# Moving the pooling additions of the values from VectorE to GpSimd in an attention and feed-forward kernel

## The chip, the cores and the metric

The kernel runs on one core of one Trainium2 chip. The metric is device time in microseconds, from the start of the program to its end. The kernel before takes 893.63 us, the median of three runs between 892.76 and 893.68 us. Engines are named as the profile names them: PE (TensorE), DVE (VectorE), ACT (ScalarE), POOL (GpSimd) and SP (SyncE, which only issues DMAs here).

## The reference

Inputs are q, k and v of shape 8 x 8 x 576 x 64 (batches, heads, positions, width of a head), and two weight matrices of 512 x 2048 and 2048 x 512.

```
k_p = k.reshape(B, H, Sp, 8, D).mean(axis=3)        # 72 pooled keys per head
v_p = v.reshape(B, H, Sp, 8, D).mean(axis=3)        # 72 pooled values per head
scores = scale * matmul(q, k_p^T); attn = softmax(scores)
x = matmul(attn, v_p)                               # laid out as 4608 tokens x 512
h = x @ w_in;  g = h * clip(h + 3, 0, 6) / 6;  out = g @ w_out
```

The step that the change is about is the mean over 8 neighbouring positions of the values: 72 pooled positions, each the sum of 8 rows of 64 numbers. (A factor of 1/8 is put in later.)

## The kernel before, in words

The 4608 tokens are cut into twelve blocks. The feed-forward part of a block fills PE almost without a pause: first the products with w_in (lines L841 and L1134), then the gate on ACT and DVE (L849 to L861, L1090 to L1098), then the products with w_out (L872, L1188, L1261), whose inputs are split in a high and a low part (L1113 on ACT, L1115 on DVE). Blocks 0 to 3 run one by one; from block 4 on, two blocks at a time form a super block, which streams its weights from DRAM (`chunk`, L980 to L994, seven buffers, five chunks ahead). Attention for a later block is done in small steps in between (`Paced`, L893 to L916): the next block's x has to be there when its turn comes.

Attention of a tile of 128 tokens and four heads takes this chain: the scores (PE, L463), their maximum (DVE, L467), four exponentials with sums (ACT, L472), the inverse of the sums (DVE, L489 and L490), the division (POOL, `divide`, L501 and L507), the transposition of the result (PE, L572 and L574), copies out of PSUM (ACT L583, L596, DVE L585, L598), and at last the product with the pooled values (PE, `av`, L646).

A batch's values are prepared by `side_steps(b)`: six loads (`load_v`), two for each of three pieces, and three calls of `prep_v(b, p)` with p = 0, 2 and 4. The pieces with p = 0 and 2 hold the first 64 pooled positions of two pairs of heads (128 partitions); the piece with p = 4 holds the remaining 8 positions of all heads (96 partitions, three small loads from `vr_l` for each half). The two halves x and y of a piece are 512 numbers per partition each. `prep_v` makes three additions, each of which reads what the one before it wrote: x += y (512 numbers), then the left half of x gets the right half added (256), then once more (128). After that ACT writes the high part of the pooled values (L395 for p = 0 and 2, L409 for p = 4) and DVE the low part (L396, L410). The loads go into a ring of four buffers, shared with the keys (`ring`, L163); a load waits until the operations that read the buffer before are done.

Two things set the order of the work. The text `ORDER` fixes each engine's order for the part of the program up to the start of block 1, in which no value of batch 2 or later is pooled. Behind it a scheduler places each instruction in its engine's queue; `mark` and `after_mark` keep side work on an engine behind the main chain's last marked instruction there. `mark` is called behind instructions of DVE, ACT and SP, and behind none of POOL. Each engine works through its queue in order, so an instruction that waits holds up all behind it.

Of the kernel before, what the change touches and what calls it, by code (L numbers as in the profile page):

```python
# [13 lines left out]
ALU = mybir.AluOpType  # L14
# [84 lines left out]
def attention_moe_kernel(  # L99
# [19 lines left out]
    nc = tc.nc  # L119
# [63 lines left out]
    def after_mark():  # L183

        if len(window) == 2 and traced[-1].engine in marks:
            behind(traced[-1], marks[traced[-1].engine])
# [141 lines left out]
    class FirstValues:  # L328
# [19 lines left out]
        def place_heads(self):  # L348
            for h in range(2):
                rows = slice(h * D, (h + 1) * D)  # L350
                nc.scalar.mul(self.v32[rows, :, h * D : (h + 1) * D], self.ps[rows], 1.0 / POOL)
# [14 lines left out]
    def place_v(b):  # L366

        W[b] = (
            pool.tile([P, NPAIR, 2 * D], F32R, name="vhi", bufs=2),
            pool.tile([P, NPAIR, 2 * D], F32R, name="vlo", bufs=2),  # L370
            pool.tile([3 * REM, NG, 4 * D], F32R, name="vrem", bufs=2),
        )
        for w in W[b][:2]:
            nc.gpsimd.memset(w.bitcast(F32), 0.0)

    def prep_v(b, p):

        if p == 0 and b not in W:
            place_v(b)
        n = P if p < NPAIR else 3 * REM  # L380
        x, y = (vraw.pop((b, p + i))[:n, : POOL * D].rearrange("p (c n) -> p c n", c=2) for i in range(2))
        for w, a, c in ((4 * D, x, y), (2 * D, x, x[:, :, 2 * D :]), (D, x, x[:, :, D:])):
            nc.vector.tensor_tensor(out=x[:, :, :w], in0=a[:, :, :w], in1=c[:, :, :w], op=ALU.add)  # L383
            after_mark()
        if p < NPAIR:
            place_heads(b, x[:, :, :D], slice(p, p + 2))
        else:
            place_rest(b, x[:, :, :D])
# [16 lines left out]
    def place_rest(b, vs):  # L405
        lo = slice(REM, 2 * REM)
        for h in range(4):
            to, own = W[b][2][:, :, h * D : (h + 1) * D], mask[:NR, 2 + h : 3 + h]
            nc.scalar.mul(to, vs[:NR], own)  # L409
            nc.vector.scalar_tensor_tensor(  # L410
                out=to[lo],
                in0=vs[lo],
                scalar=own[lo],
                in1=to[lo].bitcast(F32),
                op0=ALU.mult,
                op1=ALU.subtract,
            )
# [238 lines left out]
    def side_steps(b):  # L656

        ks = [lambda p=p: load_k(b, p) for p in range(NPAIR)]
        ks += [lambda p=p: prep_k(b, p) for p in range(NPAIR)]
        vs = []  # L660
        n = NPAIR + NG
        for p in range(n):
            vs.append(lambda p=p: load_v(b, p))
            if p > 2 and p % 2:
                vs.append(lambda p=p: prep_v(b, p - 3))
        vs.append(lambda: prep_v(b, n - 2))
        return ks, vs
# [635 lines left out]
    a = [Step(first, f, 0, 2) for f in range(SPLIT)]  # L1303
# [33 lines left out]
    b = [Scores(t, g) for g in range(NG) for t in B]  # L1337
# [229 lines left out]
```

## Time and profile before

| | before |
|---|---|
| median of the runs | 893.63 us (892.76 to 893.68) |
| the profiled execution | 893.88 us |
| its span, first to last instruction | 892.1 us |
| TensorE clock granted | 1.00 |

The profiled execution is 0.25 us over the median, and 1.8 us of it lie outside the span. The rows of the trace that the prediction uses are shown there. A row of a group gives its number of instructions, their busy time in us and the mean of one in ns; behind the second bar stands how long the engine sat idle just before them, and what ended that. A row of a line gives minimum, median and maximum in ns. A row of the timeline gives start and length in us from the span's start, and in square brackets the idle time before. A row of waits gives the sum in us, how often, and the longest.

### The profile page before, as it was taken

How to read it: one execution, taken by the hardware profiler on the slowest of the kernel's cores; microseconds unless marked ns; L12 is line 12 of the kernel's file. 1: busy time of each engine (PE TensorE's matmuls, PEld its weight loads, DVE VectorE, ACT ScalarE, POOL GpSimd, SP SyncE). 2: the span in 40 equal slices, each digit the busy share in tenths (PEclk: the TensorE clock that was granted, in tenths of full speed). 3: DMA queues.
4: the chain of work that ended last, by engine and by line, in shares of the span. 5: the costliest groups of instructions: out<-in, count | busy, mean ns of one | idle time of the engine just before them, and what ended most of it. 6: DMA issues, size and time to landing. Idle time of an engine off the chain costs nothing.

```text
span 892.1 us, 15646 instructions
## 1 busy us (share of the span) xinstructions
PE 869.2 (97%) x5360; PEld 812.3 (91%) x5360; DVE 665.9 (75%) x1340; ACT 553.6 (62%) x1515; POOL 83.6 (9%) x168
## 2 busy tenths in 40 slices
PE   7899999999999999999999999999999999999998
PEld 6788888988989998998888999999999999999998
DVE  6999864567877785869788688897597877466664
ACT  5998766655656655778344688665577746355442
POOL 4100002110211100102000101100100200000000
PEclk9999999999999999999999999999999999999999
DMA  9970205995425234996587968877976777877873
GB/s 294 392 293 1 72 24 192 360 327 167 130 67 160 71 129 135 368 315 225 180 271 239 383 218 295 265 239 236 331 250 213 226 233 240 275 253 238 266 264 132
DMA packets 124654, 200.00 MB, mean 224 GB/s; under 512 B 13216, under 2 KB 81056, under 8 KB 124576
## 3 DMA queue, kind: packets, MB, share of 16 engines
q1 hardware_dynamic: 124432, 199.00, 67.8%
q8 instruction: 43, 0.70, 0.3%
q14 instruction: 35, 0.29, 0.1%
q10 hardware_dynamic: 144, 0.00, 0.0%
HBM read 158.08 MB, written 40.89 MB: 223 GB/s over the span
## 4 chain that ended last, share of the span: by engine, by line
PE 80%; DVE 8%; DMA 5%; ACT 4%; issue 2%; SPq 1%; POOL 0%; DVEq 0%; ACTq 0%; POOLq 0%
PE psx L1134 22%; PE psx L1261 19%; PE pso L872 12%; PE psh L841 12%; PE psx L1188 7%; PE psa L646 3%; PE psa L463 3%; ACT e L472 2%; PE psa L572 1%; DMA raw<-w_in_l 1%; DMA raw<-w_out_l 1%; DMA wd<-wq 1%; DVE vst L383 1%; DMA wsFalse<-wd 1%; DVE wq L939 1%
## 5 line engine op out<-in xcount | busy, mean ns | idle before, releaser
L1134 PE MATMUL psx<-x,wsFalse 128*128 128x384 f32 x768 | 151.8, 341 | 1.7 <-DVE g L1098 0.8
L841 PE MATMUL psh<-xhi,w 128*128 128x384 f32 (+2 forms) x520 | 145.9, 340 | 0.5 <-DVE g L853 0.4
L1134 PEld LDWEIGHTS psx<-x,wsFalse 128*128 128x128 f32 x768 | 133.6, 188 | 3.2 <-ACT c L1107 1.3
L1113 ACT CAST part<-g 128x768 fp32r<-128x768 f32 x100 | 83.3, 836 | 85.0 <-PE psx L1261 65.8
L1115 DVE TENSOR_TENSOR part<-g,part 128x768 fp32r<-128x768 f32 x100 | 95.2, 955 | 46.5 <-ACT part L1113 46.1
L872 PE MATMUL pso<-w,ghi 128*128 128x512 f32 x384 | 120.7, 398 | 0.4 <-ACT o L877 0.4
L1134 PE MATMUL psx<-x,wsTrue 128*128 128x384 f32 x576 | 115.8, 342 | 2.4 <-DMA wsTrue<-wd 2.3
L1261 PE MATMUL psx<-wsFalse,part 128*128 128x256 f32 x864 | 108.3, 282 | 1.5 <-DVE part L1115 1.1
L1261 PEld LDWEIGHTS psx<-wsFalse,part 128*128 128x128 f32 x864 | 105.2, 189 | 2.3 <-DVE part L1115 1.3
L1134 PEld LDWEIGHTS psx<-x,wsTrue 128*128 128x128 f32 x576 | 99.6, 188 | 3.1 <-DVE g L1092 3.1
L841 PEld LDWEIGHTS psh<-xhi,w 128*128 128x128 f32 x520 | 93.2, 188 | 8.2 <-DVE g L853 1.1
L472 ACT ACTIVATE e<-psa,mx 128x72 f32<-128x72 f32 x256 | 78.6, 324 | 23.7 <-DVE mx L467 22.4
L841 PE MATMUL psh<-xlo,w 128*128 128x384 f32 (+2 forms) x260 | 87.1, 336 | 0.0
L501 POOL TENSOR_TENSOR a<-e,sm 128x256 f32<-128x256 f32 x60 | 41.0, 683 | 478.3 <-DVE sm L490 377.9
L1261 PE MATMUL psx<-wsTrue,part 128*128 128x256 f32 x648 | 81.3, 283 | 0.0
L1261 PEld LDWEIGHTS psx<-wsTrue,part 128*128 128x128 f32 x648 | 79.3, 191 | 0.2 <-DVE part L1115 0.2
L872 PEld LDWEIGHTS pso<-w,ghi 128*128 128x128 f32 x384 | 69.1, 188 | 11.2 <-ACT o L877 0.7
L1090 ACT ACTIVATE r<-g,small 128x384 f32<-128x384 f32 x96 | 58.8, 621 | 28.4 <-DVE g L1098 28.0
L872 PE MATMUL pso<-w,glo 128*128 128x512 f32 x192 | 74.4, 399 | 0.0
L1098 DVE TENSOR_TENSOR g<-psx,c 128x384 f32<-128x384 f32 x96 | 52.3, 553 | 28.7 <-PE psx L1134 20.6
L1107 ACT COPY c<-psx 128x384 f32<-128x384 f32 x96 | 45.0, 485 | 28.5 <-PE psx L1134 28.1
L1092 DVE SCALAR_TENSOR_TENSOR g<-r,g 128x384 f32<-128x384 f32 x96 | 54.5, 576 | 9.7 <-ACT r L1090 9.2
(139 smaller groups left out, 1473.2 us busy)
## 6 DMA issues: line engine op xcount, KB each, us to landing
wsFalse<-wd SPq DMA_DIRECT2D x64, 512.0 KB, 4.6
wsTrue<-wd SPq DMA_DIRECT2D x48, 512.0 KB, 4.9
wsFalse<-w2d SPq DMA_DIRECT2D x31, 512.0 KB, 5.0
wsFalse<-w2t SPq DMA_DIRECT2D x27, 512.0 KB, 5.0
wsTrue<-w2d SPq DMA_DIRECT2D x21, 512.0 KB, 5.0
wsTrue<-w2t SPq DMA_DIRECT2D x21, 512.0 KB, 4.9
raw<-w_in_l SPq DMA_DIRECT2D x16, 512.0 KB, 8.6
raw<-w_out_l SPq DMA_DIRECT2D x16, 512.0 KB, 9.2
```

The lines of the kernel that those rows point to most:

```text
L472: nc.scalar.activation(self.e[:, h], self.ps[:, h], AF.Exp, bias=self.mx[:, h : h + 1], accum_out=self.sm[:, h : h + 1])
L841: nc.tensor.matmul(self.ps, l[f][:, c, :], r[:, c, :], start=c == 0 and i == 0, stop=c == NCC - 1 and i == 2)
L872: nc.tensor.matmul(pos, l, r, start=f == 0 and i == 0, stop=f == NF - 1 and i == 2)
L1090: nc.scalar.activation(r, src, AF.Relu, bias=half_low, scale=GSCALE / (6.0 * WSCALE))
L1092: nc.vector.scalar_tensor_tensor(out=g_of[i][:, k], in0=r, scalar=GSCALE, in1=src, op0=ALU.min, op1=ALU.mult)
L1098: nc.vector.tensor_tensor(out=g_of[i][:, k], in0=ps, in1=kept, op=ALU.add)
L1107: nc.scalar.copy(c, ps)
L1113: nc.scalar.copy(t[:, 0], src)
L1115: nc.vector.tensor_tensor(out=t[:, 1], in0=src, in1=t[:, 0].bitcast(F32), op=ALU.subtract)
L1134: nc.tensor.matmul(ps, w[:, l, c * P : (c + 1) * P], t[:, r, c], start=o in (1, 2, 5) and c == 0 and k == 0, stop=c == 1 and k == 2, skip_ ...
L1188: nc.tensor.matmul(to, l, w[:, qs, r], start=f == 0 and k == 0, stop=end and k == 2)
L1261: nc.tensor.matmul(to, t[:, l, k, i * P : (i + 1) * P], w[:, k, r], start=begin and k == 0 and y == 0 and i % 2 == 0, stop=m == NM - 1 and ...
```

## The change: which engine makes the additions

For batches 3 to 7 (b > 2) the three additions of `prep_v` are given to POOL, and not to DVE. Batch 0 has its own code, batch 1 is pooled by `pool_second`, and batch 2 goes on as before. These are 5 batches with 3 pieces of 3 additions, 45 instructions. Nothing else in the text changes. Lines behind L383 have a number greater by one in the changed kernel (the addition is L384, the division L502, a product with the pooled values L647).

```
         for w, a, c in ((4 * D, x, y), (2 * D, x, x[:, :, 2 * D :]), (D, x, x[:, :, D:])):
-            nc.vector.tensor_tensor(out=x[:, :, :w], in0=a[:, :, :w], in1=c[:, :, :w], op=ALU.add)
+            engine = nc.gpsimd if b > 2 else nc.vector
+            engine.tensor_tensor(out=x[:, :, :w], in0=a[:, :, :w], in1=c[:, :, :w], op=ALU.add)
             after_mark()
```

Since POOL has no mark, `after_mark` ties these additions to nothing. The scheduler moves other instructions too, on all engines, from the place on where batch 3 is pooled.

The first place is POOL's queue where the values of batch 6 (the seventh) are pooled, around the place where the super block of blocks 6 and 7 goes over from its products with w_in to those with w_out. `vst` is a buffer of values, `a` and `ar` are what a division writes, `qt` a buffer of queries that is cleared. Before:

```order
L240 MEMSET qt 128x4x64
L501 TENSOR_TENSOR a<-e,sm 128x256
L507 TENSOR_TENSOR ar<-e,sm 128x64
L501 TENSOR_TENSOR a<-e,sm 128x256
L507 TENSOR_TENSOR ar<-e,sm 128x64
L501 TENSOR_TENSOR a<-e,sm 128x256
L507 TENSOR_TENSOR ar<-e,sm 128x64
L240 MEMSET qt 128x4x64
```

And after the change:

```order
L384 TENSOR_TENSOR vst<-vst 128x512
L384 TENSOR_TENSOR vst<-vst 128x2x128
L384 TENSOR_TENSOR vst<-vst 128x2x64
L240 MEMSET qt 128x4x64
L502 TENSOR_TENSOR a<-e,sm 128x256
L508 TENSOR_TENSOR ar<-e,sm 128x64
L502 TENSOR_TENSOR a<-e,sm 128x256
L508 TENSOR_TENSOR ar<-e,sm 128x64
L384 TENSOR_TENSOR vst<-vst 96x512
L384 TENSOR_TENSOR vst<-vst 96x2x128
L384 TENSOR_TENSOR vst<-vst 96x2x64
L502 TENSOR_TENSOR a<-e,sm 128x256
```

The additions of the piece p = 2 stand ahead of the clearing and two divisions, those of the remainder (96 partitions) ahead of the third division.

The second place is PE's queue a little later, where the first product with batch 6's values is made (`psx` is a sum of the feed-forward part, `psa` one of attention, `vrem` holds the remainder's pooled values). Before:

```order
L646 MATMUL psa<-ahi,vhi 128x384
L646 MATMUL psa<-alo,vhi 128x384
L646 MATMUL psa<-ahi,vlo 128x384
L1261 MATMUL psx<-wsTrue,part 128x256 x36
L1261 MATMUL psx<-wsFalse,part 128x256 x22
L646 MATMUL psa<-arem,vrem 128x384
L1261 MATMUL psx<-wsFalse,part 128x256 x15
```

And after the change:

```order
L647 MATMUL psa<-ahi,vhi 128x384
L647 MATMUL psa<-alo,vhi 128x384
L647 MATMUL psa<-ahi,vlo 128x384
L1262 MATMUL psx<-wsTrue,part 128x256 x19
L647 MATMUL psa<-arem,vrem 128x384
L1262 MATMUL psx<-wsTrue,part 128x256 x17
L1262 MATMUL psx<-wsFalse,part 128x256 x24
```

The product with the remainder stands 19 matmuls of the feed-forward part behind the first three, and not 58. On DVE the four low parts of the remainder (L410, now L411) stand ahead of the last three gates of the super block, and before they stood behind these and three splits. On SP the remainder's second half is loaded five loads of weights earlier in the queue.

The third place is PE's queue in block 3, where a tile's scores (L463, now L464) and the transposition of the same tile (L572, now L573) stand. Before, 24 matmuls of L841, 11 of L872 and 4 of other tiles' scores stand between the two; the last twelve rows of it are

```order
L872 MATMUL pso<-w_431,glo 128x512
L841 MATMUL psh<-xhi,w_614 128x384
L841 MATMUL psh<-xlo,w_614 128x384
L841 MATMUL psh<-xhi,w_614 128x384 x2
L841 MATMUL psh<-xlo,w_614 128x384
L841 MATMUL psh<-xhi,w_614 128x384 x2
L841 MATMUL psh<-xlo,w_614 128x384
L841 MATMUL psh<-xhi,w_614 128x384 x2
L841 MATMUL psh<-xlo,w_614 128x384
L841 MATMUL psh<-xhi,w_614 128x384
L872 MATMUL pso<-w_486,ghi 128x512 x2
L572 MATMUL psa<-ident,a 128x128 x2
```

After the change these rows are all that stands between the tile's scores and its transposition, with the transposition as the last:

```order
L842 MATMUL psh<-xlo,w_344 128x384
L842 MATMUL psh<-xhi,w_344 128x384 x2
L842 MATMUL psh<-xlo,w_344 128x384
L842 MATMUL psh<-xhi,w_344 128x384
L842 MATMUL psh<-xlo,w_486 128x384
L842 MATMUL psh<-xhi,w_486 128x384 x2
L842 MATMUL psh<-xlo,w_486 128x384
L842 MATMUL psh<-xhi,w_486 128x384 x2
L842 MATMUL psh<-xlo,w_486 128x384
L842 MATMUL psh<-xhi,w_486 128x384
L464 MATMUL psa<-kbd_84,qt 128x144 x4
L573 MATMUL psa<-ident,a 128x128 x2
```

These are 13 matmuls of the feed-forward part and 4 of scores.

## Prediction

> **What bounds the kernel now.** I read the page first.
>
> ```profile
> span 892.1 us, 15646 instructions
> PE 869.2 (97%) x5360; PEld 812.3 (91%) x5360; DVE 665.9 (75%) x1340; ACT 553.6 (62%) x1515; POOL 83.6 (9%) x168
> PE 80%; DVE 8%; DMA 5%; ACT 4%; issue 2%; SPq 1%; POOL 0%; DVEq 0%; ACTq 0%; POOLq 0%
> ```
>
> PE bounds it: it is busy in 869.2 of 892.1 us, and the change takes no matmul away. All that it can win is idle time of PE, 22.9 us, and of that only what comes of DVE and lies where the values of batch 3 and later are pooled. So the second view is the waits of PE. I leave out those of the first 45 us, which the change doesn't reach.
>
> ```profile
> PE psx L1134 <- DMA wsTrue<-wd: 2.3, 1, 2.3
> PE psa L463 <- DVE arem L598: 1.3, 3, 0.9
> PE psx L1261 <- DVE part L1115: 1.1, 1, 1.1
> PE psx L1134 <- DVE g L1098: 0.8, 1, 0.8
> PE psa L646 <- DVE alo L585: 0.7, 3, 0.3
> PE psa L572 <- POOL a L501: 0.7, 1, 0.7
> PE psh L841 <- DVE g L853: 0.4, 1, 0.4
> ```
>
> The longest, 2.3 us, is a load of weights, which the change doesn't touch. The five rows with DVE hold 4.3 us: this is the whole prize. The third view, the timeline at these waits, tells whether the additions on DVE cause them. Here is DVE at the first one,
>
> ```profile
> 414.99 0.68 DVE L383 TENSOR_TENSOR vst<-vst 128x512 f32<-128x512 f32 x1
> 416.48 0.69 DVE L383 TENSOR_TENSOR vst<-vst 96x512 f32<-96x512 f32 x1 [0.81 <-DMA vst<-vr_l]
> 417.40 0.29 DVE L598 TENSOR_TENSOR arem<-psa,arem 32x128 fp32r<-32x128 f32 x1
> ```
>
> and PE there and at two others:
>
> ```profile
> 417.74 0.76 PE L463 MATMUL psa<-kbd,qt 128*128 128x144 f32 x4 [0.90 <-DVE arem L598]
> 564.43 0.96 PE L1134 MATMUL psx<-x,wsFalse 128*128 128x384 f32 x4 [0.84 <-DVE g L1098]
> 581.63 2.04 PE L1261 MATMUL psx<-wsFalse,part 128*128 128x256 f32 x15 [1.07 <-DVE part L1115]
> ```
>
> At 417.74 PE waits 0.90 us for a low part that DVE could not make, since an addition ahead of it stood 0.81 us for its load and then took 0.69 us. The other two lie beside the additions of batch 6:
>
> ```profile
> 561.08 1.10 DVE L383 TENSOR_TENSOR vst<-vst 128x512 f32<-128x512 f32 x1
> 563.04 0.41 DVE L383 TENSOR_TENSOR vst<-vst 128x256 f32<-128x256 f32 x1
> 572.31 0.69 DVE L383 TENSOR_TENSOR vst<-vst 96x512 f32<-96x512 f32 x1 [3.57 <-DMA vst<-vr_l]
> 579.46 1.13 DVE L410 SCALAR_TENSOR_TENSOR vrem<-vst,small,vrem 32x128 fp32r<-32x128 f32 x4
> ```
>
> The wait of 0.84 us follows two additions of 1.51 us together in DVE's queue. The one of 1.07 us comes 9 us after DVE stood still for 3.57 us with a load, with the splits that PE needs queued behind.
>
> **The change, part by part.** *What DVE loses.* The additions by shape:
>
> ```profile
> L383 DVE TENSOR_TENSOR vst<-vst 128x512 f32<-128x512 f32 x12 | 9.1, 762 | 0.1
> L383 DVE TENSOR_TENSOR vst<-vst 128x256 f32<-128x256 f32 x12 | 5.0, 418 | 0.1
> L383 DVE TENSOR_TENSOR vst<-vst 128x128 f32<-128x128 f32 x12 | 3.4, 284 | 0.0
> L383 DVE TENSOR_TENSOR vst<-vst 96x512 f32<-96x512 f32 x6 | 4.1, 684 | 4.4 <-DMA vst<-vr_l 4.4
> ```
>
> Three additions of 128 partitions are 0.76 + 0.42 + 0.28 = 1.46 us; 10 such pieces and 5 of 96 partitions (about as long) make some 15 x 1.46 = 21.9 us off DVE's 666. The waits for loads, 4.4 us in two places, both of batches 5 and 6, go from DVE to POOL as well. Since PE is the bound, the 21.9 us count only through the waits above.
>
> *What POOL gains.* The nearest additions of POOL are those of batch 0, on 32 partitions, and the divisions:
>
> ```profile
> L357 POOL TENSOR_TENSOR stage<-stage x3: 447/715/1252, 11.9 to 14.8; 32x512 f32<-32x512 f32 x1, 32x256 f32<-32x256 f32 x1, 32x128 f32<-32x128 f32 x1
> L501 POOL TENSOR_TENSOR a<-e,sm x60: 612/614/1313, 130.2 to 704.1; 128x256 f32<-128x256 f32 x60
> ```
>
> Upper end: 1.25 + 0.72 + 0.45 = 2.41 us a piece. Lower end: the division's 614 ns for 256 numbers, taken as 0.6 for 256, 1.2 for 512 and 0.3 for 128, gives 2.15. I take 2.41, from the same operation: 15 x 2.41 = 36 us, on an engine that is busy for 84 of 892. A piece's chain grows by 2.41 - 1.46 = 0.95 us.
>
> *Who waits for the longer chain.* For batches 3, 4, 5 and 7 nobody, I think: a batch's values are used some microseconds after they are there. Batch 6 is the close one; it is a rival below. Behind the additions in POOL's queue stand the divisions, which lead to a transposition on PE; an addition that waits for its load would hold them up. For batch 6 POOL has room:
>
> ```profile
> 545.59 0.39 SPq L284 DMA_DIRECT2D vst<-v_l  x1
> DMA to landing us min/median/max: 1.8/4.5/8.6
> 558.30 0.31 POOL L240 MEMSET qt<- 128x256 f32 x1 [11.28 <-PE psa L463]
> ```
>
> The last load of the piece p = 2 is issued at 545.59 and lands about 550.1 (median 4.5 us). DVE begins to add at 561.08, because of its queue; POOL is idle for 11.28 us before 558.30 and can add at once. The ring's buffer comes free sooner, so the load of the remainder, which waits for it, is issued sooner too, as SP's new order has it. On SP the weights of five loads stand behind that one; they are asked for five chunks ahead (18 matmuls each, at 2.04 / 15 = 0.136 us about 2.4 us, so 12 us), which hides a wait of a few.
>
> *The shared lock.* Does POOL slow DVE down? The trace shows that it does, with operations that read two inputs from SBUF:
>
> ```profile
> 635.50 0.61 POOL L501 TENSOR_TENSOR a<-e,sm 128x256 f32<-128x256 f32 x1 [3.93 <-ACT r L1090]
> 635.52 1.01 DVE L1092 SCALAR_TENSOR_TENSOR g<-r,g 128x384 f32<-128x384 f32 x1 [0.18 <-ACT r L1090]
> L1092 DVE SCALAR_TENSOR_TENSOR g<-r,g x96: 522/556/1012, 354.9 to 828.6; 128x384 f32<-128x384 f32 x96
> L1092 DVE SCALAR_TENSOR_TENSOR g<-r,g 128x384 f32<-128x384 f32 x96 | 54.5, 576 | 9.7 <-ACT r L1090 9.2
> L1098 DVE TENSOR_TENSOR g<-psx,c x96: 527/557/560, 352.3 to 827.3; 128x384 f32<-128x384 f32 x96
> ```
>
> A gate that starts 0.02 us after a division lasts 1.01 us where the median is 0.556; L1098, which has one of its inputs in PSUM, never exceeds 0.560. All 96 gates lose 96 x (0.576 - 0.556) = 1.9 us. With 36 us more of POOL they and the splits lose a few more, far less than the 21.9 us that DVE is freed of. For PE's share I bound it by 0 and by one long addition in full, 1.25 us, at a place where PE waits for DVE, and take 0.5.
>
> [...]
>
> *The scheduler's new order.* At the third place of the change's rows, a tile's transposition moves close to its scores. In the trace that tile's chain runs so:
>
> ```profile
> 276.55 0.68 PE L463 MATMUL psa<-kbd,qt 128*128 128x144 f32 x4
> 280.43 0.61 POOL L501 TENSOR_TENSOR a<-e,sm 128x256 f32<-128x256 f32 x1 [17.50 <-DVE sm L490]
> ```
>
> What PE has between the two is in the new order 13 matmuls of L841, which the chain of waits shows with their time,
>
> ```profile
> 339.52 2.10 PE psh L841 x12
> ```
>
> and 0.65 us of other scores: 13 x 2.10 / 12 + 0.65 = 2.9 us. The scores end at 277.23, the division at 281.04: 3.8 us. It waits 0.9 us if the chain is as slow as this, nothing if it is 2.9 us; I take 0.7, since only queueing on DVE can be saved.
>
> **The sum**, from the profiled execution's 893.88 us: the wait of 0.90 goes (-0.90), that of 0.84 goes (-0.84), that of 1.07 half, as DVE now has the remainder's low parts (L410) ahead of the gates and still waits for the load (-0.54), the gate's 0.4 half (-0.20); the transposition +0.7, the lock +0.5. Together -1.3: 892.6. The profiled execution is 0.25 us over the median of 893.63, so the runs' median becomes 892.4. About 0.2%, 1.8 us, is what a measurement can tell from no change; the forecast lies within it.
>
> **The rivals.** *All DVE waits go.* DVE is freed of 21.9 us and of 4.4 us of waiting at loads, and new waits don't come: -0.90 - 0.84 - 1.07 - 0.4 = -3.2 us, 890.4; with L585's 0.7 889.7. For it: in each of the places additions stand ahead. Against: the scheduler used the room to move attention forward.
>
> *The remainder of batch 6 comes too late* (slower). The matmuls ahead of PE's product with it, and the low part (ACT's share of it) that the product reads:
>
> ```profile
> 572.85 4.68 PE L1261 MATMUL psx<-wsTrue,part 128*128 128x256 f32 x36
> 576.62 1.28 ACT L409 ACTIVATE vrem<-vst,small 96x128 fp32r<-96x128 f32 x4 [0.80 <-DVE vst L383]
> ```
>
> The product now stands 19 matmuls of 4.68 / 36 = 0.13 us behind 572.85, at about 575.3. In the trace DVE's first low part is there at 579.46 + 1.13 / 4 = 579.7. If the load comes no sooner and the chain takes 0.95 us longer, PE waits 5.4 us, 4.3 more than the 1.07 that it replaces: 898.0 by the median; half of it gives 895.8. It decides when the load lands: the additions take 2.41 us, ACT's round and DVE's first low part 1.28 + 0.28 = 1.6, so it must land before 571.3, 1.0 us sooner than DVE's wait ended (572.31). Against it: POOL can add p = 2 ten microseconds sooner.
>
> *The lock* (slower). If every long addition holds a gate or split for all its time, DVE loses 36 us for 21.9 saved. Where it is nearly full, that shows:
>
> ```profile
> 240.00:260.00 20.00, 19.30 (x105) 17.19 (x104) 17.85 (x54) 12.78 (x52) 3.71 (x6) 1.00 0.29 74
> ```
>
> The pairs are busy time and instructions of PE, PEld, DVE, ACT and POOL: DVE has 2.15 us of slack there; two pieces add 1.9 us net and eat it. I price it at 1 us in this stretch and in the next like it (360 to 380 us): +2.2 with what the gates lose elsewhere, 895.8. The point is 2 us more DVE time in such a stretch.
>
> **How the numbers follow.** Forecast 0.42 (892.4, own range 891.9 to 894.5); all waits go 0.38; the remainder 0.12; the lock 0.08. So faster 0.38, same 0.42, slower 0.20. The range reaches from 889.7 of the second case to 896.0, past both slower cases at their halves.
>
> **What would show it.** Right: POOL near 120 us, DVE near 645 to 650, no DVE wait for `vr_l`, PE's waits at 417, 564 and 581 gone or smaller, the transposition near 280 waiting for POOL by under 1 us, L1092 with more long ones. Wrong: PE waiting over 2 us at the remainder's product near 575; additions of 512 numbers far from 1.25 us; DVE's sum not falling; or another wait for weights.

## The result, and the profile after

The changed kernel is slower: 898.13 us in the median of 7 runs (896.36 to 900.50), against 893.63 us in 7 runs of before (891.55 to 895.72). The ratio is 1.0059, with a 95% interval of 1.0044 to 1.0074, so 3.9 to 6.6 us lost. The forecast was 892.4 us, in a range of 889.7 to 896.0. Its profiled execution took 896.36 us, the fastest of the seven.

The first lines of the page after:

```profile
span 894.6 us, 15588 instructions
PE 871.3 (97%) x5360; PEld 813.5 (91%) x5360; DVE 663.3 (74%) x1295; ACT 553.1 (62%) x1515; POOL 125.1 (14%) x213
```

POOL has 41.5 us more, but DVE is only 2.6 us below the 665.9 of before, though 45 additions have left it. And PE, which has the same matmuls, is busy for 2.1 us longer. The two have different causes. DVE's first: these are the groups by shape (count, then busy time and mean in ns).

```profile
L384 POOL TENSOR_TENSOR vst<-vst 128x512 f32<-128x512 f32 x10 | 13.6, 1363 | 36.6 <-DMA vst<-v_l 17.6 <-DVE g L1093 8.6 <-DVE wq L945 8.1
L384 POOL TENSOR_TENSOR vst<-vst 128x256 f32<-128x256 f32 x10 | 9.6, 961 | 0.6
L384 POOL TENSOR_TENSOR vst<-vst 128x128 f32<-128x128 f32 x10 | 5.4, 537 | 0.7
L1093 DVE SCALAR_TENSOR_TENSOR g<-r,g 128x384 f32<-128x384 f32 x96 | 62.2, 657 | 11.6 <-ACT r L1091 11.2
```

The 96 gates with two inputs in SBUF take 657 ns on average, 576 before: 7.8 us more on DVE. Other operations of DVE have grown too; summed one by one, all that stayed on it takes 13.2 us more than before. POOL's additions are longer too, 2.86 us for three and not 2.41. So the two engines hold each other up far more than forecast: 14 of the 96 gates took over 0.75 us, and the three additions on 96 partitions that POOL began at 414.52 us took 4.11. Does that cost time? The main waits of PE behind the first 45 us:

```profile
PE psx L1135 <- DMA wsTrue<-wd: 1.7, 1, 1.7
PE psx L1135 <- ACT c L1108: 1.5, 3, 0.6
PE psa L647 <- DVE alo L586: 1.3, 2, 1.0
PE psa L573 <- POOL a L502: 1.2, 2, 0.7
PE psx L1135 <- ACT o L878: 1.0, 1, 1.0
PE psa L464 <- DVE arem L599: 0.9, 1, 0.9
PE psa L647 <- ACT e L473: 0.8, 1, 0.8
PE psx L1135 <- DVE g L1099: 0.6, 1, 0.6
PE psa L647 <- DVE arem L599: 0.4, 1, 0.4
```

The wait for `part` at 581 us is gone, as is that of a score for `arem` at 417 us. In their place stand others, most of them short. Three lie together, in the timeline of PE just behind 419 us, at the products with batch 4's values:

```profile
420.42 0.33 PE L647 MATMUL psa<-ahi,vhi 128*128 128x192 f32 x1 [1.02 <-DVE alo L586]
...
421.76 0.36 PE L647 MATMUL psa<-ahi,vhi 128*128 128x192 f32 x1 [0.79 <-ACT e L473]
...
422.79 0.48 PE L647 MATMUL psa<-arem,vrem 96*128 96x192 f32 x2 [0.45 <-DVE arem L599]
```

Now the same place by windows (the first pair is PE's busy time, and the number before the last two is the granted clock):

```profile
419.70:423.11 3.41, 1.45 (x8) 1.12 (x8) 3.28 (x11) 2.84 (x13) 0.00 (x0) 1.00 0.46 148
423.11:426.53 3.42, 3.31 (x11) 2.97 (x10) 3.33 (x9) 1.81 (x5) 1.58 (x2) 0.50 0.00 0
426.53:429.94 3.41, 3.41 (x19) 2.87 (x19) 2.79 (x8) 0.75 (x4) 0.00 (x0) 1.00 0.46 154
```

PE is busy for 1.45 of 3.41 us, and for the next 3.41 us its clock is halved: half of that, 1.7 us, is lost. That is most of PE's 2.1 us more of busy time. The sum of the two profiled executions: in the first 45 us PE idles 1.6 us less than in before (loads that the change doesn't touch), behind them 2.0 us more (12.1 against 10.0, summed over the gaps between its matmuls), and 1.7 us go to the clock. That is 2.1 of the 2.5 us between the spans. The mean clock of the other six runs is 0.994 to 0.996, where the profiled one has 0.998: by that, one or two more such halvings, of 0.0019 each, in all of them.

### The profile page after: what moved, and what is told of

Read it like the earlier page. It is cut to its first block, busy times and chain, and to the rows that moved or that the text cites. A ratio compares the mean times of both kernels' runs of the same rounds, so it can differ in the third digit from the quotient of the medians.

```text
span 894.6 us, 15588 instructions
## 1 busy us (share of the span) xinstructions
PE 871.3 (97%) x5360; PEld 813.5 (91%) x5360; DVE 663.3 (74%) x1295; ACT 553.1 (62%) x1515; POOL 125.1 (14%) x213
## 4 chain that ended last, share of the span: by engine, by line
PE 81%; DVE 9%; DMA 4%; ACT 3%; issue 1%; SPq 1%; POOL 0%; DVEq 0%; ACTq 0%; POOLq 0%
PE psx L1135 21%; PE psx L1262 20%; PE psh L842 12%; PE pso L873 12%; PE psx L1189 7%; PE psa L647 4%; PE psa L464 3%; DMA wd<-wq 2%; DVE g L1093 1%; ACT e L473 1%; PE psa L573 1%; DMA kst<-k_l 1%; DVE g L1099 1%; DMA wsFalse<-wd 1%; SPq L949 1%
## 5 line engine op out<-in xcount | busy, mean ns | idle before, releaser
L502 POOL TENSOR_TENSOR a<-e,sm 128x256 f32<-128x256 f32 x60 | 39.7, 662 | 410.8 <-DVE sm L491 372.6
L1099 DVE TENSOR_TENSOR g<-psx,c 128x384 f32<-128x384 f32 x96 | 52.3, 554 | 28.5 <-PE psx L1135 17.9
L1093 DVE SCALAR_TENSOR_TENSOR g<-r,g 128x384 f32<-128x384 f32 x96 | 62.2, 657 | 11.6 <-ACT r L1091 11.2
```

The source lines that it names most:

```text
L1093: nc.vector.scalar_tensor_tensor(out=g_of[i][:, k], in0=r, scalar=GSCALE, in1=src, op0=ALU.min, op1=ALU.mult)
L1099: nc.vector.tensor_tensor(out=g_of[i][:, k], in0=ps, in1=kept, op=ALU.add)
```

## The experiments

The two suspects came in together. POOL now adds, and the scheduler made another order. To take them apart the order was written out: each queue is held in a list's order behind block 0, by the same kind of tie that `put_in_order` uses, which adds no wait. The edit, with the lists themselves left out:

```
     if ORDER:
         put_in_order()
+        keep_order(traced[window[1]:], behind)
...
+def keep_order(instructions, behind):
+    for name, text in LATER.items():
+        engine = getattr(mybir.EngineType, name)
+        mine = [i for i in instructions if i.engine == engine and (i.opcode == "DMACopy") == (name == "SP")]
...
+        for x, y in zip(numbers, numbers[1:]):
+            behind(mine[y], mine[x].name)
+LATER = {"PE": ...
```

All runs at a glance. The ratio is against runs of before on the same chip. "Idle" is PE's idle time behind the first 45 us of the profiled execution, in us. The mean clock is that of all runs of the kernel; that of before was 0.9980 to 0.9995 in the four groups of runs that list it.

| kernel | additions on POOL | order | ratio (95% interval) | clock | idle |
|---|---|---|---|---|---|
| before | none | its own | 1 | | 10.0 |
| changed | 45 | scheduler | 1.0059 (1.0044 to 1.0074) | 0.9960 | 12.1 |
| order_before_adds_pool | 45 | before | 0.9960 (0.9946 to 0.9974) | 0.9990 | 7.6 |
| order_after_adds_dve | none | changed | 1.0047 (1.0029 to 1.0065) | 0.9974 | 13.8 |
| after_pe_filled | 45 | changed | 1.0028 (1.0015 to 1.0042) | 0.9992 | 13.2 |
| order_before_rest_pool | 15 | before | 0.9964 (0.9951 to 0.9977) | 0.9992 | 8.3 |
| order_before_heads_pool | 30 | before | 1.0012 (0.9997 to 1.0028) | 0.9980 | 10.1 |
| order_held_to_440 | 45 | before, then scheduler | 0.9986 (0.9972 to 1.0000) | 0.9987 | 9.5 |
| scheduled_rest_pool | 15 | scheduler | 1.0076 (1.0053 to 1.0098) | 0.9942 | 14.9 |
| after_splits_later | 45 | changed but for 8 | 1.0037 (1.0019 to 1.0054) | 0.9968 | 13.4 |
| rest_pool_splits_later | 15 | scheduled_rest_pool's but for 8 | 1.0008 (0.9993 to 1.0023) | 0.9975 | 10.2 |
| scheduled_heads_pool | 30 | scheduler | 1.0066 (1.0046 to 1.0085) | 0.9972 | 13.9 |
| adds_dve_untied | none | scheduler | 1.0074 (1.0048 to 1.0100) | 0.9977 | 14.8 |
| adds_pool_tied | 45 | scheduler | 1.0086 (1.0067 to 1.0105) | 0.9923 | 14.3 |

**order_before_adds_pool**: the changed kernel with `LATER` holding the order of before.

> The additions of batches 3 to 7 on POOL as in the change, but behind block 0 every queue (PE, DVE, ACT, SP) is held in the order that the kernel before has; in POOL's queue each addition stands where DVE began it in the trace of before. Theory A (the scheduler's new order costs the time: it bunches the products with batch 4's values near 420 us, PE idles there and its clock is halved for a while): with the old order the loss is gone, 892 to 894.5 us, about as before, granted clock like that of before. Theory B (POOL's additions hold DVE's operations up, which makes the splits and gates late for PE): the loss stays, 896 to 899 us; the gates with two inputs in SBUF (L1093, 657 ns on average after the change, 576 before) stay above 630 ns and DVE's sum near 663 us.

890.99 us against 894.61: ratio 0.9960, faster than before by 3.6 us and, by the ratios, than the changed kernel by about 9. And the gates are as slow as after the change:

```profile
L1093 DVE SCALAR_TENSOR_TENSOR g<-r,g 128x384 f32<-128x384 f32 x96 | 62.0, 655 | 10.3 <-ACT r L1091 9.6
...
L384 POOL TENSOR_TENSOR vst<-vst 96x512 f32<-96x512 f32 x5 | 6.9, 1374 | 8.4 <-DMA vst<-vr_l 8.4
```

POOL stands 8.4 us at the loads of the remainder, and PE waits for none of it. The stretch in question, PE nearly full and its clock at 1.00:

```profile
400.00:420.00 20.00, 19.74 (x126) 19.12 (x125) 17.98 (x44) 17.30 (x69) 12.93 (x18) 1.00 0.78 241
420.00:440.00 20.00, 20.00 (x98) 16.60 (x97) 15.36 (x32) 9.16 (x23) 2.82 (x6) 1.00 0.59 189
```

So the engine of the additions is not what costs the time, and what DVE loses beside POOL (8 us in the gates alone) does not keep this order from being faster than before. Theory A holds, though the time lies below the 892 to 894.5 us expected.

**order_after_adds_dve**: the kernel before, with `LATER` holding the order of after; the additions are on DVE, and `after_mark` is left out behind those of batches 3 to 7 (the list sets their place).

> The other half: the additions stay on DVE, but every queue is held in the order of the changed kernel, each addition standing in DVE's queue where POOL began it in the trace after. Theory A (order): as slow as the changed kernel, 896.5 to 899 us, PE's waits near 420 us add up to 2 us or more and the clock drops there. Theory B (POOL holds DVE up): 892.5 to 895 us; the gates with two inputs in SBUF come back to about 576 ns and the first wait near 420 us (1.02 us, for the low part of a transposition) falls below 0.5 us, since the operations ahead of it lose the 1.0 us that they stood still beside POOL's additions.

899.14 us, ratio 1.0047: as slow as the changed kernel within the intervals, with nothing on POOL. The gates are back at 578 ns, and the three waits are there, the first of them shorter, as B said:

```profile
425.47 0.33 PE L647 MATMUL psa<-ahi,vhi 128*128 128x192 f32 x1 [0.45 <-DVE alo L586]
...
426.77 0.36 PE L647 MATMUL psa<-ahi,vhi 128*128 128x192 f32 x1 [0.75 <-ACT e L473]
...
427.83 0.47 PE L647 MATMUL psa<-arem,vrem 96*128 96x192 f32 x2 [0.48 <-DVE arem L599]
```

POOL's hold on DVE is thus worth about 0.6 us at the first of them (1.02 to 0.45). The stretch as a whole is no shorter for it: just ahead PE stands 0.77 and 0.33 us for gates of DVE, which it does not in the changed kernel. What A forecast in detail is there in part: the three waits alone add up to 1.7 us, not to 2 (2.8 with the two ahead of them), and in the profiled execution the clock dropped between 360 and 380 us (0.91 over that stretch), behind a wait of 2.8 us for weights, and not here (1.00 from 420 to 440 us).

**after_pe_filled**: the changed kernel in its own order, with work for the idle PE.

```
     def av(j, b, x0, T, p, later=None):
         ps = att_bank()[:, :T]
+        if (j, b) == (7, 4) and p < 2:
+            for _ in range(3):
+                nc.tensor.matmul(ps[:, :P], ident, ident, start=True, stop=True)
```

> The changed kernel in its own order, with three idle products of the unit matrix ahead of each of the two first products with batch 4's values near 420 us (about 0.2 us each, into a bank that the product overwrites); nothing waits for them and PE stands idle there anyway. Theory C (PE's idling itself halves the clock for a window of 3.4 us, which costs about 1.7 us each time): the clock is 1.00 in the stretch 420 to 440 us (0.91 after the change) and the median falls by 1 to 1.7 us, to 896.4 to 897.2 us. If the clock drops for another reason, or the idle time does not matter: 0.91 again and 897.8 to 898.6 us, since at most 0.3 us of work is added to the path.

897.06 us, ratio 1.0028, and a mean clock of 0.9992 instead of 0.9960. In the stretch 420 to 440 us the clock is 1.00. The first group of idle products did not help, since it had to wait as long as the product behind it; the second filled the gap behind (the trace has two instructions for each product):

```profile
423.24 0.91 PE L647 MATMUL psa<-ident 128*128 128x128 f32 x6 [1.05 <-DVE alo L586]
...
424.58 0.94 PE L647 MATMUL psa<-ident 128*128 128x128 f32 x6
...
420.00:440.00 20.00, 18.70 (x100) 15.83 (x99) 16.07 (x35) 10.36 (x31) 3.93 (x6) 1.00 0.51 155
```

Work that computes nothing makes the kernel faster by 0.0031 of 894, 2.8 us. That is more than the 1 to 1.7 us expected. The gain in the clock, 0.0032 of the time, is as much, so about half of the loss goes with the clock. One halving is 0.0019; where the rest of this gain comes from is not shown, since of each kernel one execution alone has a trace. The rest, 2.5 us against a before whose own clock was 0.9980, is idle time.

**order_before_rest_pool** and **order_before_heads_pool**: which additions carry the gain, in the order of before. The edits to the line of the engine:

```
+            engine = nc.gpsimd if b > 2 and p == NPAIR else nc.vector
```

```
+            engine = nc.gpsimd if b > 2 and p < NPAIR else nc.vector
```

> Order of before in every queue, and only the remainder's additions (15 instructions, the ones whose loads DVE waits 4.4 us for) on POOL. Theory A1 (with the order held, what is won is DVE's standing still at the loads of the remainder, with the splits behind it): most of the gain of the full version with the order held (0.996 of before) is there, ratio 0.9955 to 0.9975, and PE's waits of 0.90 us at 417 and 1.07 us at 581 are gone. Theory A2 (what is won is DVE's room, 21.9 us of additions): a third of it or less, ratio 0.9985 to 1.0.

> The complement: order of before, only the additions on 128 partitions (30 instructions) on POOL; the remainder's stay on DVE, with their waits at loads. Theory A1: little of the gain, ratio 0.998 to 1.0; the wait of 0.84 us at 564 goes, those at 417 and 581 stay. Theory A2: two thirds of the gain, ratio 0.9965 to 0.998. In both the gates with two inputs in SBUF are slower than the 576 ns of before, 620 to 645 ns on average.

0.9964 and 1.0012: theory A1 (the second a little above the range on record, within its interval). The 15 additions of the remainder bring all of the gain, and the 30 others none. What those 30 win they lose again: the wait of 0.84 us for a gate at 564 us goes, and at 562 us comes one for a division that stands behind an addition in POOL's queue (POOL, and then PE):

```profile
560.11 1.28 POOL L384 TENSOR_TENSOR vst<-vst 128x512 f32<-128x512 f32 x1
561.36 0.93 POOL L502 TENSOR_TENSOR a<-e,sm 128x256 f32<-128x256 f32 x1
```

```profile
562.34 0.44 PE L573 MATMUL psa<-ident,a 128*128 128x128 f32 x2 [0.79 <-POOL a L502]
```

order_before_adds_pool has the same wait with 0.80 us, and with the remainder's additions alone on POOL it is absent. With the 30 on POOL the wait at 581 us is still 0.71 us, and at 417 us DVE still stands at the remainder's load, with a low part queued behind it (DVE, and then PE; the row names a load of weights, but what landed just ahead of it, at 415.88 us, is the remainder's last part):

```profile
416.10 0.69 DVE L384 TENSOR_TENSOR vst<-vst 96x512 f32<-96x512 f32 x1 [1.63 <-DMA wsFalse<-w2d]
416.71 0.28 DVE L586 TENSOR_TENSOR alo<-psa,ahi 128x128 fp32r<-128x128 f32 x1
417.02 0.29 DVE L599 TENSOR_TENSOR arem<-psa,arem 32x128 fp32r<-32x128 f32 x1
```

```profile
417.37 0.76 PE L464 MATMUL psa<-kbd,qt 128*128 128x144 f32 x4 [2.04 <-DVE arem L599]
```

So the change wins by taking a wait from DVE, not by taking work from it.

**order_held_to_440**: the order of before for what began by 440 us, and the scheduler free behind that (each later instruction is tied behind the last of the list).

> All 45 additions on POOL; the queues are held in the order of before up to what began by 440 us in its trace, behind that the scheduler is free. If the loss of the changed kernel lies in the stretch of 215 to 440 us (PE's waits near 350 and 420 us and the halved clock behind them): ratio 0.995 to 0.9985. If it lies behind 440 us (waits near 560 to 570 and 703 us): ratio 1.0015 to 1.005.

0.9986: most of the loss lies ahead of 440 us, as the first case says, though just outside its range. About 2.3 us against the fully held order (0.0026) lie behind it: four waits of 0.4 to 0.6 us between 556 and 564 us and one of 1.2 us at 700 us, both also in the changed kernel.

**scheduled_rest_pool**: the 15 additions that bring the gain, and the scheduler free. The line of the engine is that of order_before_rest_pool; nothing holds the order.

> The change for the remainder's additions alone (b > 2 and the piece p = 4), and the scheduler free, as in the changed kernel: a third of the instructions move, and 932 places in PE's queue differ from before. Theory A (the order decides, and it changes with any small edit): the time can differ from that of the same additions with the order held by 2 us or more, either way, 889 to 899 us, and where it is slower the trace shows new waits of PE between products with the values, and the clock under 1. Theory B (POOL's load decides): it agrees with the version with the order held within 1 us.

901.04 us, ratio 1.0076: 10 us slower than the same additions in the order of before. B is off by far more than its 1 us, and the time lies above the range that A gave. Here the order's harm can be read in one piece, from POOL over ACT to PE:

```profile
420.87 2.59 POOL L384 TENSOR_TENSOR vst<-vst 96x512 f32<-96x512 f32 x3 [3.31 <-DMA wsFalse<-w2d]
```

```profile
423.50 1.28 ACT L410 ACTIVATE vrem<-vst,small 96x128 fp32r<-96x128 f32 x4 [3.25 <-POOL vst L384]
424.80 0.48 ACT L1108 COPY c<-psx 128x384 f32<-128x384 f32 x1
```

```profile
425.33 1.97 PE L1135 MATMUL psx<-x,wsTrue 128*128 128x384 f32 x5 [3.97 <-ACT c L1108]
...
420.00:440.00 20.00, 16.03 (x73) 14.16 (x72) 13.49 (x32) 9.38 (x30) 4.78 (x7) 0.83 0.47 151
```

The high parts of batch 5's remainder stand in ACT's queue ahead of a copy. They wait 3.25 us for POOL, which had waited for the remainder's load (its last part landed at 420.57 us, just ahead of the addition, though the row names a load of weights), and behind them waits the copy that PE needs: PE idles 3.97 us, and the clock is halved for the next 6.8 us (0.83 over 20 us). In the order of before, the copy (L1107) and four exponentials (L472) stand ahead of them; ACT's queue in that order:

```
L1107 COPY c<-psx 128x384
L596 CAST arem<-psa 64x64
L472 ACTIVATE e,sm<-psa,mx 128x72 x4
L395 ACTIVATE vhi<-vst 64x2x64 x2
L409 ACTIVATE vrem<-vst,small 96x2x64 x4
```

and in that of the changed kernel, where the exponentials stand behind:

```
L1108 COPY c<-psx 128x384
L410 ACTIVATE vrem<-vst,small 96x2x64 x4
L1091 ACTIVATE r<-psx,small 128x384
L597 CAST arem<-psa 64x64
L473 ACTIVATE e,sm<-psa,mx 128x72 x4
```

**rest_pool_splits_later** and **after_splits_later**: the same two orders, in which only eight instructions move, the four high parts on ACT and the four low parts on DVE. In the lists their numbers stand behind those of the exponentials on ACT, and behind those of L586 (first kernel) or L599 (second) on DVE.

> The version in which only the remainder's additions are on POOL and the scheduler was free (ratio 1.0076), in its order but for the same eight instructions: the four high parts on ACT stand behind the copy (L1108) and the four exponentials that they stood ahead of, where ACT sat idle 3.25 us for POOL and PE 3.97 us for the copy; the four low parts on DVE stand behind the next low part of a transposition (L586). Theory D: that wait of PE falls from 3.97 to under 1 us and the 6.8 us of half clock behind it go (3.4 us), 6 us or more together: ratio 1.000 to 1.002, mean clock 0.998 or more. If the wait only moves to another place: 1.005 to 1.009.

1.0008 instead of 1.0076. Eight instructions further back in their queues are worth 6 us. The copy is made 4.7 us earlier, ahead of the splits, and PE's stretch is whole again:

```profile
420.06 0.48 ACT L1108 COPY c<-psx 128x384 f32<-128x384 f32 x1 [0.57 <-PE psx L1135]
...
423.55 1.28 ACT L410 ACTIVATE vrem<-vst,small 96x128 fp32r<-96x128 f32 x4
```

```profile
420.00:440.00 20.00, 19.52 (x98) 16.16 (x97) 15.67 (x37) 10.22 (x31) 4.66 (x7) 1.00 0.58 182
```

The mean clock rose to 0.9975, short of the 0.998 on record.

> The changed kernel in its own order, but for eight instructions: the four high parts of batch 5's remainder on ACT (L410) stand behind the four exponentials (L473) that they stood ahead of near 419 us, and their four low parts on DVE (L411) behind the low part of a transposition (L599) near 423.9 us, about where they are in the order of before. Theory D (in the scheduler's new order the splits, not the additions, stand ahead of what PE waits for): of PE's waits near 420 us (1.02, 0.79 and 0.45 us) the second and third go, the first stays (it hangs on DVE's gates); PE's idling no longer fills a window and the clock stays at 1.00 there. Together 1 us of waits and up to 1.7 us of clock: ratio 1.0028 to 1.0042 against 1.0059 for the change. If the place of these splits doesn't matter: 1.005 to 1.007.

1.0037, in the forecast range, but its interval overlaps that of the change, and the mechanism is there by halves only. The third wait is gone, the second is 0.57 us, and in the profiled execution the clock still dropped. (Nor had PE's idling filled a window there in the changed kernel: PE was busy for 1.45 of the 3.41 us ahead of the half clock.)

```profile
422.69 0.33 PE L647 MATMUL psa<-ahi,vhi 128*128 128x192 f32 x1 [1.08 <-DVE alo L586]
...
423.81 0.35 PE L647 MATMUL psa<-ahi,vhi 128*128 128x192 f32 x1 [0.57 <-ACT e L473]
...
420.00:440.00 20.00, 18.35 (x87) 15.42 (x86) 16.36 (x36) 9.73 (x30) 3.46 (x5) 0.91 0.48 139
```

Theory D is shown for the first kernel and is at most part of the story for the changed one.

**scheduled_heads_pool**: the 30 other additions, and the scheduler free.

> The additions on 128 partitions alone on POOL (b > 2 and p < 4), the scheduler free; with the order of before held, this set gave a ratio of 1.0012. Its queue of ACT has the high parts of batch 5's remainder ahead of the four exponentials, as the changed kernel has; before had them behind. Theory A with D: slower than the held version by 2 us or more, ratio 1.0035 to 1.007, with PE waits near 420 us and a clock below 0.998. If the order does not matter: 1.000 to 1.0025.

1.0066, against 1.0012 with the order held: theory A again, with one wait of 2.31 us near 420 us and the clock at 0.91 there. It is not the wait of theory D: PE waits for a gate (L1099), and ahead of that gate in DVE's queue stands the remainder's first addition. DVE sat idle for 1.62 us before it and began it at 418.09 us, just behind the landing of its load (417.92 us).

**adds_dve_untied**: no addition changes its engine.

```
             nc.vector.tensor_tensor(out=x[:, :, :w], in0=a[:, :, :w], in1=c[:, :, :w], op=ALU.add)
-            after_mark()
+            if b < 3:
+                after_mark()
```

> The kernel before with one edit that changes no engine: for batches 3 to 7 the call of after_mark behind the additions is left out, so that the scheduler may put them anywhere in DVE's queue; the change does the same in passing, since POOL has no marks. The scheduler is free. Its order differs from before in 1080 places of PE's queue, and ACT's queue has the high parts of batch 5's remainder ahead of the four exponentials near 420 us, as the changed kernel has. Theory A (the order decides, and losing the tie is what changes it): slower than before though nothing is on POOL, ratio 1.003 to 1.008, clock below 0.998. If POOL is needed for the loss: 0.9985 to 1.002.

1.0074, with the gates at 574 ns. Untying the additions is enough for a loss of this size, with nothing on POOL; the change unties them in passing, because POOL has no marks. The order that comes of it is a third one, though, neither that of before nor that of the changed kernel.

**adds_pool_tied**: the opposite. All 45 on POOL, and each tied behind DVE's last mark.

```
-    def after_mark():
+    def after_mark(of=None):
...
-        if len(window) == 2 and traced[-1].engine in marks:
-            behind(traced[-1], marks[traced[-1].engine])
+        if len(window) == 2 and (of or traced[-1].engine) in marks:
+            behind(traced[-1], marks[of or traced[-1].engine])
...
-            after_mark()
+            after_mark(nc.vector.engine if b > 2 else None)
```

> All 45 additions on POOL as in the change, but tied for the scheduler behind DVE's last marked instruction, as the additions on DVE are (a tie without a wait); the scheduler is free otherwise. Its order has the four exponentials near 420 us ahead of the remainder's high parts, as before has. Theory A with D: the loss at 420 us goes, ratio 0.996 to 1.001, PE's waits near 420 us under 1 us together. If the tie does not matter: 1.004 to 1.0075, as the change.

1.0086, the slowest of all, and the expectation failed: the exponentials do stand ahead of the splits, and PE still waits 4.26 us at 427 us. Here POOL's hold on DVE lies on the path (POOL, then DVE):

```profile
419.38 5.92 POOL L384 TENSOR_TENSOR vst<-vst 96x512 f32<-96x512 f32 x6 [2.36 <-DMA vst<-vr_l]
```

```profile
419.91 2.46 DVE L1093 SCALAR_TENSOR_TENSOR g<-r,g 128x384 f32<-128x384 f32 x2
422.29 0.28 DVE L586 TENSOR_TENSOR alo<-psa,ahi 128x128 fp32r<-128x128 f32 x1
422.49 1.44 DVE L490 TENSOR_SCALAR sm<-sm 128x4 f32<-128x4 f32 x1
```

Six additions in a row on POOL, and beside them two gates take 2.46 us where two at the median of 556 ns take 1.1, and an operation on 4 numbers per partition takes 1.44 us where its 72 take 0.198 on average after the change. The four low parts of the remainder (L411), which stand ahead of the gate too, take 1.72 us and not 1.13. That is 3.2 us of DVE ahead of the gate that PE waits for. So the tie back is no cure: it gave another order with a fault of its own. That the hold makes most of these 4.26 us is argued from the rows; no run took it away in this order.

## Why the prediction was wrong

**The step that failed is "The scheduler's new order".** It priced the order by one transposition, at +0.7 us. That wait didn't come; the transposition runs right behind the scores ahead of it:

```profile
276.25 1.14 PE L464 MATMUL psa<-kbd,qt 128*128 128x144 f32 x8
277.37 0.44 PE L573 MATMUL psa<-ident,a 128*128 128x128 f32 x2
```

The new order costs 0.0047 of the time without POOL (order_after_adds_dve), and between the two orders with all additions on POOL lie 0.0099, about 9 us. The order was looked at in three places picked beforehand; what was found of the loss sits elsewhere, at products with batch 4's values, and in steps that merely changed places with the splits.

**The clock was taken as 1.00 throughout,** as the page of before has it. A group of short waits was priced at their sum. In the changed kernel the three near 420 us (1.02, 0.79 and 0.45 us) were followed by 3.42 us at half clock, 1.7 us more; with the idle products in one gap, the runs gained 2.8 us.

**What DVE loses: the sum was mis-sized.** The 21.9 us are durations added up; the additions overlap their neighbours in the trace of before, and without them DVE's busy time there is 15.8 us less. The other operations then grew by 13.2 us, which leaves 2.6, where "a few" were forecast. The lock rival's condition, DVE losing nearly what it saves, came true, and its price didn't: with the order held the same loss goes with a gain of 3.6 us. At the one wait where it was taken away the hold was worth 0.6 us. That the sum had 0.5 is luck: it was the author's estimate, picked between 0 and 1.25, for one place.

**What POOL gains** was 43.6 us, not 36 (the six groups of L384). The shortest of each shape make 2.47 us a piece, 37 us in all, so the size was right for undisturbed additions; the rest comes of those that lasted longer beside DVE (4.11 us for the three from 414.52 us on).

**The waits.** That of 0.90 at 417 us and that of 1.07 at 581 us went, 0.84 at 564 us became 0.59, 0.48 and 0.57 us in a row, and the gate's 0.4 at 256 us went. In the order of before, "all DVE waits go" is nearly what happened: 890.99 us, 3.6 below before where 3.2 to 3.9 were priced. That the number fits is in part luck: the gate's wait stayed, 0.80 us for a division came, PE's idle time fell by 2.4 us (10.0 to 7.6), and some 0.9 us is the clock (0.9980 to 0.9990), which no case priced. This rival was right about where the gain lies, and had 0.38; it had the scheduler as its only objection, and that was the point.

**The remainder of batch 6** was there in time, and its product did not wait:

```profile
579.16 0.34 PE L647 MATMUL psa<-arem,vrem 96*128 96x384 f32 x1
```

The mechanism that this rival named, steps that stand in a queue behind POOL's late additions, did decide in scheduled_rest_pool, at batch 5's remainder and by ACT's queue, which the prediction did not look at.

**What stays open.** Of the 9 us between the two orders, the clock is some 2.7 us (0.9960 to 0.9990) and idle time 4.5 in the profiled executions (12.1 and 7.6); the rest is not accounted for. In the changed kernel the idle time is spread over ten waits of 0.4 to 1.0 us from 230 to 703 us, beside one for weights; only those near 420 us were tried singly, and each scheduler order has its own set. No run holds the order of before with nothing else changed, so that the holding itself is free is not shown; the nearest is order_before_heads_pool with 1.0012. Nor does a run show why all five free orders are worse than that of before, which may simply be an unusually good one.

## What to carry to other kernels

Where a scheduler places the instructions, an edit is two changes: the one that was meant, and a new order. Five different edits with the scheduler free were all slower than before, by 0.6 to 0.9%, one of them with no engine changed; with the order of before held, three of them ran from 0.4% faster to no different. So hold the order and measure the edit alone, and look in every engine's queue at what has moved ahead of the steps that PE waits for. Waits for loads are better taken by an engine behind whose queue nothing urgent stands: 15 additions that stood at loads were worth all of the gain, and 30 others nothing.

## What the runs showed of the hardware

**Behind short waits, PE's clock was halved.** In the changed kernel's profiled execution PE was busy for 1.45 of the 3.41 us ahead of 423.11 us, and from there to 426.53 us the granted clock as the trace records it was 0.50. With the idle products in a gap (after_pe_filled) it was 1.00 from 420 to 440 us, where the changed kernel has 0.91, and the mean of all runs was 0.9992 and not 0.9960. The changes of the clock that the trace of the changed kernel records lie at 6.69, 423.11, 426.53 and 894.15 us, 122, 1 and 138 times 3.413 us apart; the two that the trace of before records, at 6.16 us and, behind the span's end, at 893.62 us, 260 times. Ahead of 894.15 us, where the clock was halved too, PE was busy for 0.26 of 3.41 us. Three other steps of these two traces have PE busy for about half (1.67 and 1.70 of 3.41 us in before, from 9.57 and 886.80 us on, and 1.74 in the changed kernel from 10.10 us on), and behind them the clock stayed at 1.00. Idle time over a longer stretch does not tell it: from 340 to 360 us PE was busy for 17.66 of 20 us in before, 17.60 in after_splits_later and 16.23 in rest_pool_splits_later, and from 360 to 380 us the clock was 1.00, 0.91 and 1.00. The seven runs of the changed kernel have mean clocks of 0.998, 0.996 and 0.994; at 0.0019 for each halving these would be one, two and three of them, an estimate, since one of the seven alone has a trace.

**The longest gates ended just behind an operation of POOL.** The longest gate is 1.66 us where the median is 0.558, and three additions of POOL on 128 partitions took 2.86 us, those on 32 partitions 2.41. In the changed kernel 14 of the 96 gates took over 0.75 us. Each of them began while an addition or a division ran on POOL, and ended 0.41 to 0.42 us after that one's end. With the additions on DVE in the same order (order_after_adds_dve) the gates took 578 ns on average and not 657. In adds_pool_tied an operation on 4 numbers per partition, `sm<-sm`, took 1.44 us beside the additions, where the 72 of the changed kernel take 0.198 us on average. What the two engines share there, no row shows; "the lock" is the prediction's name for it.
